# Attention with decay and a bilinear FFN on one core: idle matmuls at the start, f loaded through ScalarE's queue, eight transposes of P moved from DMA to the tensor engine, a new order

## The chip, the core and the metric

The kernel runs on one core of one Trainium2 chip. The core has a tensor engine (PE; its weight loads are shown apart as PEld), a vector engine (DVE), a scalar engine (ACT), GpSimd (POOL) and SyncE (SP), which issues most DMAs; 16 DMA engines move the data. The metric is the device time of one execution in microseconds (us); lower is better.

## What is computed

Forgetting attention over 8 batches of 8 heads, 576 tokens each, head dimension 64, then a bilinear FFN on the 4608 tokens:

```python
scores = scale * np.matmul(q, k.transpose(0, 1, 3, 2))
log_f = np.log(np.clip(f, 0.0001, 1.0))
cum = np.cumsum(log_f, axis=-1)
decay = cum[:, :, :, None] - cum[:, :, None, :]
scores = np.where(causal, -1000000000.0, scores + decay)
attn = softmax(scores)                       # max, exp, sum, divide
out  = np.matmul(attn, v)                    # 8 x 8 x 576 x 64
x = out.transpose(0, 2, 1, 3).reshape(4608, 512)
a = x @ w_a                                  # 512 x 1536
b = x @ w_b
return a * b @ w_out                         # 1536 x 512
```

The inputs are float32 in HBM (q, k, v, f, w_a, w_b, w_out); the kernel works in fp16 on PE with float32 sums.

## The kernel before

Two heads make a pair; t = 0 to 31 counts the pairs, four to each batch b. Queries and keys of a pair are cut into blocks of 128 (i = 0 to 3) and a last block of 64 (i = 4). The work is written as a list of small operations, each with one engine, the operations it needs and a function that emits its instructions. The order in which they are emitted is not worked out at run time: it is a list of operation numbers (`ORDER`) with a letter for each operation that more than one engine could do (`CHOICE`). Each engine runs its own instructions strictly in that order, and so does each DMA queue.

- **Start.** `f_load` (L170) loads f in two DMAs on SP's queue. `constants` (L72) makes an identity matrix `ident16` on POOL (L73) and then masks and selection vectors. `clip`, the logarithm (ScalarE, L212), `scan` (L187) and the copies into `crow` turn f into the running sum of log f, in two pieces of columns. q and k of batch 0 are loaded (L270), cast to fp16 (L242, L244), transposed by PE against the identity (`pe_transpose`, L285; PSUM tile `psT`) and copied out by DVE or ACT (`pe_evict`). v is loaded at L251 and cast into `nv`.
- **Scores.** `qk_group` (L417) multiplies q and k blocks into PSUM tile `sc`. For batch 0 the decay and the mask are added by matmuls (`crow`, `pick`, `neg`, `low`); for later batches the decay is added on DVE (L540) from `spread`. For pairs 4 to 7 PE broadcasts the decay (`spread_mm`, L482, tile `scd`: one 128x512 matmul each); later pairs load it by DMA (L493).
- **Softmax.** DVE takes the maxima (L514 in batch 0), ACT the exponentials (L567, L571), DVE the reciprocals (L579, L581), POOL the products P times 1/sum (L589). P of a pair lies in `PA` (blocks i = 0 to 2; for the first two batches in two parts, A0 for i = 0, 1 and A1 for i = 2, six 128x128 blocks each) and `PB` (i = 3, 4).
- **Transposes of P.** In batch 0 (`PEP`) PE transposes P (`pe_tr`, L609, tile `psP`) and DVE or ACT copies it out (`pe_tr_evict`). From batch 1 on a DMA does it (`do_tr`, L603, on SP's queue). For the first two batches the transposed A parts lie in the later half of `xT`, a buffer that is free until then; so `xT<-PA` in the profile is such a transpose.
- **P times V.** `do_pv` (L631) and `do_pv4` (L647) into tile `pv` (one buffer), copied to `xT`.
- **FFN.** Cuts of tokens: 256, 256, 256, 384, then 512 each. `ff_mm` (L914) makes `psa` and `psb` in 12 blocks, ACT copies `psa`, DVE multiplies (L925), `ff_out` (L934) makes `pso`, which is copied and stored (L954). A cut needs the attention of all its tokens, from all four pairs. POOL issues the weight loads (L392).

The branch that chooses between PE and DMA for the transposes is `if b in PEP:` (L822); what sets the engine order is lines 1036 to 1160.

Of the kernel before, what the change touches and what calls it, by code (L numbers as in the profile page):

```python
# [9 lines left out]
FP32 = mybir.dt.float32  # L10
# [15 lines left out]
def kernel(  # L26
# [11 lines left out]
    nc = tc.nc  # L38
# [30 lines left out]
    ident16 = perm.tile([128, 128], FP16, tag="ident16", name="ident16")  # L69
    warm = perm.tile([128, 1], FP32, tag="warm", name="warm")  # L70

    def constants():  # L72
        make_identity(nc, ident16)  # L73
        for x in pickh:
            nc.gpsimd.memset(x, 0.0)
        for m in range(4):
            x = slice(32 * m, 32 * m + 32)
# [71 lines left out]
    def take(op, tag):  # L149

        users = [op]
        op.takes.append((tag, users))
        return users
# [16 lines left out]
    def f_load(half):  # L170
        rows = f.rearrange("b (h p) s -> h b p s", h=2)
        nc.sync.dma_start(out=cw["f"][64 * half:64 * half + 32, :], in_=rows[half])
# [27 lines left out]
    o_f = [Op("SP", 0.5, lambda _, half=half: f_load(half), prio=-310, land=0.3, name=f"ldf{half}") for half in range(2)]  # L200
# [3 lines left out]
    o_c = Op("POOL", 4.5, lambda _: constants(), prio=-300)  # L204
# [99 lines left out]
    PEP = tuple(range(1))  # L304

# [372 lines left out]
    def attention(t, base):  # L678
# [12 lines left out]
        if not direct:  # L691
            if t in PSPREAD:
# [3 lines left out]
                for h in range(2):  # L696
                    bm = Op("PE", 512 * COLS, lambda _, h=h: spread_mm(t, h), crow_ops[0] + crow_ops[1] + [bc0] + bcs, prio=prio(0) - 5, mode="full", name=f"bm{t}")
                    su = take(bm, "ff")
                    bc = Op(None, {"ACT": 0.59, "DVE": 0.69}, lambda e, h=h: spread_ev(e, t, h), [bm, bc0], prio=prio(0) - 5, name=f"bc{t}")
                    su.append(bc)  # L700
                    bcu.append(bc)
                    bcs.append(bc)
            else:
# [115 lines left out]
        for part in norms:  # L819
            lo, hi = BLOCKS[part]  # L820
            p = prio({"A0": 0, "A1": 1}.get(part, 2))
            if b in PEP:  # L822
# [210 lines left out]
    for n in cuts:  # L1033
# [3 lines left out]
        0 1 26 20 32 38 3-6 27 28 11 7 2 29 30 12 21 22 8 10 9 13 14 19 33 34 23 24 31 25 18 61 64 35 70 106 15  # L1037
# [7 lines left out]
        178 1739 173 256 174 1741-1743 272 1740 1744 275 265 266 179 273 1745 104 139 276 289 283 282 290 105  # L1045
# [3 lines left out]
        1762-1764 280 287 60 288 221 222 226 484 264 328 385 329 293 150 330 294 472 473 231 1765 334 1766 384  # L1049
        378 339 232 373 1767 1768 379 386 233 194 1769 1771 389 390 340 388 387 485 295 234 1770 1773 341 1774  # L1050
        342 391 392 1775 336 195 1772 1776 274 296 297 393 303 304 474 1777-1779 239 298 475 299 305 1780 338
# [4 lines left out]
        1802 427-429 439 440 435 1804 313 1805 1807 1806 1809 1808 1810 314 424 434 1811 442 441 1812 1813  # L1056
# [4 lines left out]
        528 519-521 529 546 1837 545 413 414 552 1838 530-532 553 547 507 533 514 513 579 676 1786 458 671 460  # L1061
# [6 lines left out]
        608 616 594 636 617-619 614 643 644 620 637 610 684 622 609 596 621 615 1893-1896 638 645 639 646 1898  # L1068
# [10 lines left out]
        1969-1971 798 895 896 816 897 797 1972 787 788 811 794 821 822 1973 823 1974 838 1976 1978 892 836 791  # L1079
        826 827 846 847 818 1975 1977 824 828-830 907 898 903 953 848 854 856 1979 849 1980 842 839 1982 812 806  # L1080
        831 819 813 908 820 832 825 853 855 841 860 917 1983 1981 844 867 861 857 1984 1985 868 837 1986 840 850
        852 899 904 858 1987-1989 863 834 833 1990 1992 843 910 1994 869 954 905 1991 862 1996 1993 918 926 872
# [5 lines left out]
        986 955 980 987 982 1000 984 990 991 1100 992 993 951 952 2023 2018 1002 2026 2029-2031 1003 1006 2034  # L1088
# [102 lines left out]
```

## Time and profile before

| what | value |
|---|---|
| median of 3 runs | 418.04 us (415.95 to 419.21) |
| profiled execution, device time | 413.75 us |
| its span | 412.0 us |
| its granted clock of PE | 0.998 |
| PE busy | 388.2 us (94%) |
| DVE busy | 302.8 us (73%) |
| ACT busy | 277.8 us (67%) |
| POOL busy | 265.1 us (64%) |

The profile's page gives busy time by engine for one execution; "busy" for PE counts a matmul from issue to its modelled end, so neighbouring matmuls overlap. The page also cuts the span into 40 slices of 10.3 us; each digit is a tenth of the slice:

```profile
PE   1698999999999999899999999999999999999995
DVE  5987998897889859777798789768878793432331
ACT  2877898885987668876786778777877673231230
POOL 6899797877796786875967787767865845000000
```

PE is nearly full from the third slice to the end, the other three until about slice 32; what is left after that is FFN alone. A finer view of any stretch can be asked: instructions in order of time, who waited for whom, and the busy time of each engine in chosen stretches.

### The profile page before, as it was taken

The page shows a single profiled execution, that of the slowest core. Times are in us where ns is not written, and L with a number is a line of the kernel's source. Part 1 is how long each engine was busy: PE and PEld are TensorE (multiplying, and loading weights), DVE is VectorE, ACT ScalarE, POOL GpSimd, SP SyncE. Part 2 cuts the span into 40 slices and gives each one's busy share as a digit, 9 for nine tenths or more (in the row PEclk, how much of TensorE's full clock was granted, in tenths as well). Part 3 has the DMA queues.
Part 4 walks back from the last instruction along what each step waited for, and adds up shares of the span by engine and source line. Part 5 has one row for each costly group of instructions (what it writes and reads, how often), then busy time and mean ns, then how long its engine had stood idle before and what let it go on. Part 6 is the DMA issues. An engine that isn't in the chain of part 4 may idle for free. (4 is left out here: it accounts for less than half of the span.)

```text
span 412.0 us, 10863 instructions
## 1 busy us (share of the span) xinstructions
PE 388.2 (94%) x3788; PEld 209.6 (51%) x3788; DVE 302.8 (73%) x1011; ACT 277.8 (67%) x788; POOL 265.1 (64%) x490
## 2 busy tenths in 40 slices
PE   1698999999999999899999999999999999999995
PEld 1456675756756544444445444444454444444552
DVE  5987998897889859777798789768878793432331
ACT  2877898885987668876786778777877673231230
POOL 6899797877796786875967787767865845000000
PEclk9999999999999999999999999999999999999999
DMA  6999999999999999999999999996996729200102
GB/s 245 200 240 215 227 197 244 211 230 256 257 215 233 288 218 246 221 240 244 232 208 283 298 190 211 266 223 210 186 222 205 156 56 180 84 1 11 68 0 103
DMA packets 153575, 80.56 MB, mean 196 GB/s; under 512 B 130736, under 2 KB 133552, under 8 KB 153520
## 3 DMA queue, kind: packets, MB, share of 16 engines
q1 hardware_dynamic: 149616, 75.02, 78.5%
q0 software_dynamic: 3760, 4.72, 7.0%
q8 instruction: 29, 0.48, 0.5%
q14 instruction: 26, 0.21, 0.2%
q10 hardware_dynamic: 144, 0.13, 0.1%
HBM read 52.05 MB, written 9.58 MB: 150 GB/s over the span
## 5 line engine op out<-in xcount | busy, mean ns | idle before, releaser
L540 DVE CUSTOM_DVE_ANT_0 S<-sc,spread 64x576 f32<-64x576 f32 (+4 forms) x232 | 126.4, 562 | 13.3 <-PE sc L417 6.1
L914 PE MATMUL psa<-xT,wa 128*128 128x512 f16 (+2 forms) x528 | 115.3, 341 | 1.3 <-ACT a L240 0.8
L914 PE MATMUL psb<-xT,wb 128*128 128x512 f16 (+2 forms) x528 | 115.3, 341 | 0.4 <-DVE PTB L244 0.2
L240 ACT CAST a<-psa 128x512 f16<-128x512 f32 (+2 forms) x132 | 66.5, 505 | 57.2 <-PE psa L914 50.5
L925 DVE TENSOR_TENSOR ht<-psb,a 128x512 f16<-128x512 f32 (+2 forms) x132 | 77.4, 590 | 34.2 <-PE psb L914 26.3
L589 POOL TENSOR_SCALAR PA<-PA,st 128x256 f16<-128x256 f16 (+2 forms) x192 | 90.3, 480 | 18.3 <-DVE st L581 12.3
L934 PE MATMUL pso<-wout,ht 128*128 128x512 f16 x432 | 100.0, 380 | 0.0
L571 ACT ACTIVATE PA<-S,st 128x256 f16<-128x256 f32 (+2 forms) x168 | 84.6, 506 | 8.1 <-DVE st L540 8.1
L589 POOL TENSOR_SCALAR PB<-PB,st 128x512 f16<-128x512 f16 (+1 forms) x96 | 67.6, 712 | 24.3 <-DVE st L581 13.1
L914 PEld LDWEIGHTS <-wa 128*128 128x128 f16 x528 | 49.0, 98 | 42.1 <-issue 4.4
L914 PEld LDWEIGHTS <-wb 128*128 128x128 f16 x528 | 49.1, 98 | 40.2 <-issue 1.8
L934 PEld LDWEIGHTS <-ht 128*128 128x128 f16 x432 | 39.8, 98 | 45.6 <-issue 0.9
L571 ACT ACTIVATE PB<-S,st 128x512 f16<-128x512 f32 x56 | 40.4, 721 | 11.1 <-DVE st L540 9.7
L417 PE MATMUL sc<-kT,qT 64*128 64x128 f16 (+4 forms) x384 | 35.8, 274 | 3.1 <-ACT kT L240 1.4
L240 ACT COPY osb<-pso 128x512 f32<-128x512 f32 (+1 forms) x19 | 10.8, 569 | 32.3 <-DMA out_dram<-osb 15.7
L571 ACT ACTIVATION_READ_ACCUMULATOR PA<-S,st 128x1 f32 x168 | 32.3, 192 | 0.0
L244 DVE CAST xT<-pv 128x512 f16<-128x512 f32 (+1 forms) x40 | 23.1, 576 | 6.6 <-PE pv L631 6.4
L244 DVE COPY osb<-pso 128x512 f32<-128x512 f32 (+1 forms) x18 | 12.1, 674 | 20.8 <-PE pso L934 14.9
L631 PEld LDWEIGHTS <-nv 128*64 128x64 f16 x640 | 19.5, 110 | 13.1 <-issue 9.8
L581 DVE RECIPROCAL st<-st 128x2 f32<-128x2 f32 x128 | 18.9, 157 | 9.9 <-ACT PB L571 5.2
L417 PEld LDWEIGHTS <-qT 64*128 64x128 f16 (+1 forms) x384 | 13.8, 96 | 23.0 <-issue 15.6
L567 ACT ACTIVATE PB<-S,st 128x576 f16<-128x576 f32 x28 | 21.7, 775 | 4.4 <-issue 2.3
(92 smaller groups left out, 454.2 us busy)
## 6 DMA issues: line engine op xcount, KB each, us to landing
spread<-cum_d SPq DMA_DIRECT2D x24, 576.0 KB, 5.6
out_dram<-osb SPq DMA_DIRECT2D x35, 256.0 KB, 2.8
q<-in_q_dram SPq DMA_DIRECT2D x15, 576.0 KB, 6.4
k<-in_k_dram SPq DMA_DIRECT2D x15, 576.0 KB, 5.9
v<-in_v_dram SPq DMA_DIRECT2D x32, 256.0 KB, 5.7
wout<-in_moe_w_out_dram POOLq DMA_DIRECT2D x3, 512.0 KB, 7.8
v<-in_v_dram SPq DMA_DIRECT2D x8, 128.0 KB, 4.4
wa<-in_moe_w_a_dram POOLq DMA_DIRECT2D x2, 512.0 KB, 10.3
```

The costliest lines, as they stand in the source:

```text
L240: nc.scalar.copy(out=out_, in_=in_)
L244: VEC[e].tensor_copy(out=out_, in_=in_)
L417: nc.tensor.matmul(out=dst, lhsT=lhsT, rhs=rhs, start=start, stop=stop, skip_group_check=True)
L540: nc.vector.tensor_tensor_reduce(out=o, in0=x, in1=y, scale=-1.0, scalar=3e38, op0=ADD, op1=MIN, accum_out=m)
L567: nc.scalar.activation(out=p_blocks(t, 4), in_=T[("s" if direct else "z", t, 4)], func=EXP, bias=st[:, 8:9], scale=sign, accum_out=st[:, 1 ...
L571: nc.scalar.activation(out=p_blocks(t, i)[:, :, h, :], in_=(T[("s", t, i)][:, h, :] if direct else T[("z", t, i)][:, h * n:h * n + n]).rea ...
L581: nc.vector.reciprocal(out=st[:, 20 + 2 * i:22 + 2 * i], in_=st[:, 10 + 2 * i:12 + 2 * i])
L589: VEC[e].tensor_scalar(out=p, in0=p, scalar1=st[:, c:c + 1], scalar2=1.0, op0=MUL, op1=MUL)
L631: nc.tensor.matmul(out=o[HP[h], 128 * i:128 * i + 128], lhsT=vt[:, j, pr + NP * h, :], rhs=pt[:, base_blk[i] + 2 * block_at(t, i, j) + h, ...
L914: nc.tensor.matmul(out=p[:, 0:n], lhsT=w16[:, db, 128 * fb:128 * fb + 128], rhs=xTflat[db][:, t0:t0 + n], start=(db == 0), stop=(db == 3))
L925: nc.vector.tensor_tensor(out=ht[:, 0:n], in0=T.pop(("psb", t0, fb))[:, 0:n], in1=T.pop(("a16", t0, fb))[:, 0:n], op=MUL)
L934: nc.tensor.matmul(out=o, lhsT=T[("ht", t0, fb)][:, 128 * tb:128 * tb + 128], rhs=wout16[:, fb, :], start=(fb == 0), stop=(fb == 11))
```

## The change

Five things change.

1. The identity matrix becomes an operation of its own on POOL (`identity`), ahead of the other constants.
2. Twenty operations `wake` are added on PE. Each is two matmuls of 64 rows of the identity against one identity column, broadcast to 512 columns, into a tile of tag `pv`; nothing reads it. They need only the identity. In the new order six stand ahead of the first transpose of q, two more ahead of k's, two ahead of the first scores, and the other ten between the operations of batch 0, the last one ahead of the third P times V product (`pv1`).
3. f is loaded on ScalarE's queue (two DMAs ahead of everything else on ScalarE). The first load on SP's queue is now the 64-token rest of v (`ld0v4`), then q, k, k, q and v of batch 0.
4. For pairs 4 to 7 (batch 1), parts A0 and A1 are transposed by PE: eight `do_tr` go, eight `pe_tr` of six blocks with eight `pe_tr_evict` come (four on ACT, four on DVE). Part B of these pairs stays with the DMA.
5. `ORDER` and `CHOICE` are new for the whole kernel. Among the choices, one k cast of batch 0 goes from ACT to POOL, the rest of v of batch 0 (`ca0v2`) from POOL to DVE, and some evictions between DVE and ACT; the weight loads on POOL stand at other places.

The branch added for `MASKP` inside the `PSPREAD` case is never taken (pairs 4 to 7 are not in `MASKP`).

```diff
+    def identity():
+        make_identity(nc, ident16)
+
+    def wake(n):
+        x = ps.tile([128, 512], FP32, tag="pv", bufs=1, name="wake")
+        for _ in range(n):
+            nc.tensor.matmul(out=x, lhsT=ident16[0:64, :], rhs=ident16[0:64, 0:1].to_broadcast([64, 512]),
+                             start=True, stop=True, skip_group_check=True)
+
     def constants():
-        make_identity(nc, ident16)
         for x in pickh:
...
-        nc.sync.dma_start(out=cw["f"][64 * half:64 * half + 32, :], in_=rows[half])
+        nc.scalar.dma_start(out=cw["f"][64 * half:64 * half + 32, :], in_=rows[half])
...
-    o_f = [Op("SP", 0.5, lambda _, half=half: f_load(half), prio=-310, land=0.3, name=f"ldf{half}") for half in range(2)]
+    o_f = [Op("ACT", 0.85, lambda _, half=half: f_load(half), prio=-310, land=0.3, name=f"ldf{half}") for half in range(2)]
...
-    o_c = Op("POOL", 4.5, lambda _: constants(), prio=-300)
+    o_i = Op("POOL", 1.2, lambda _: identity(), prio=-301, name="ident")
+    o_c = Op("POOL", 3.3, lambda _: constants(), [o_i], prio=-300, name="const")
+    for n in range(20):
+        o = Op("PE", 0.427, lambda _: wake(2), [o_i], prio=-290, mode="row", name=f"wake{n}")
+        o.prev = [last_wake] if n else []
+        last_wake = o
+        take(o, "pv")
...
     PEP = tuple(range(1))
+    PEQ = {(t, x) for t in range(4, 8) for x in ("A0", "A1")}
...
-            if b in PEP:
+            if b in PEP or (t, part) in PEQ:
...
     ORDER = """
-        0 1 26 20 32 38 3-6 27 28 11 7 2 29 30 12 21 22 8 10 9 13 14 19 33 34 23 24 31 25 18 61 64 35 70 106 15
...
+        2 0 1 69 47 41 53 59 24-26 32 27 33 48 49 28 42 43 29 31 30 34 3-9 50 10 11 39 51 40 44 12 45 46 52 35
...
     CHOICE = """
-        DDPPDDAADDADAPDAPPDDPPPDDAADDDADDDDADDAAAAAADADDADDDDAAAAADADAAAAAAAADADDADAAAAAAADADAADADAAAADADAAA AAA
+        DDPPDDAADDAAPPDAPPDDPDPDDDADDDADADAADDAAAAAADADAAADDDAADDDDADAAAAADAAADAADDAAADDDAAAAAADAAADAAADDA
+        DAAADDDADAA
```

More of the change, by code (lines that the diff above doesn't have):

```diff
@@ L702, in attention @@
                     bcs.append(bc)
+                if t in MASKP:
+                    mc = Op("POOL", 0.9, lambda _: mask_copy(t), list(bcs), prio=prio(0) - 4, name=f"mc{t}")
+                    ml = Op("POOL", 0.42, lambda _: mask_last(t), [mc], prio=prio(3) - 0.5, name=f"ml{t}")
+                    bcu.extend([mc, ml])
             else:
@@ L1036 @@
     ORDER = """
-        0 1 26 20 32 38 3-6 27 28 11 7 2 29 30 12 21 22 8 10 9 13 14 19 33 34 23 24 31 25 18 61 64 35 70 106 15
[7 rows of a table removed]
-        178 1739 173 256 174 1741-1743 272 1740 1744 275 265 266 179 273 1745 104 139 276 289 283 282 290 105
[3 rows of a table removed]
-        1762-1764 280 287 60 288 221 222 226 484 264 328 385 329 293 150 330 294 472 473 231 1765 334 1766 384
-        378 339 232 373 1767 1768 379 386 233 194 1769 1771 389 390 340 388 387 485 295 234 1770 1773 341 1774
-        342 391 392 1775 336 195 1772 1776 274 296 297 393 303 304 474 1777-1779 239 298 475 299 305 1780 338
[4 rows of a table removed]
@@ L1056 @@
-        1802 427-429 439 440 435 1804 313 1805 1807 1806 1809 1808 1810 314 424 434 1811 442 441 1812 1813
[4 rows of a table removed]
-        528 519-521 529 546 1837 545 413 414 552 1838 530-532 553 547 507 533 514 513 579 676 1786 458 671 460
[6 rows of a table removed]
-        608 616 594 636 617-619 614 643 644 620 637 610 684 622 609 596 621 615 1893-1896 638 645 639 646 1898
[10 rows of a table removed]
-        1969-1971 798 895 896 816 897 797 1972 787 788 811 794 821 822 1973 823 1974 838 1976 1978 892 836 791
-        826 827 846 847 818 1975 1977 824 828-830 907 898 903 953 848 854 856 1979 849 1980 842 839 1982 812 806
@@ L1081 @@
-        831 819 813 908 820 832 825 853 855 841 860 917 1983 1981 844 867 861 857 1984 1985 868 837 1986 840 850
-        852 899 904 858 1987-1989 863 834 833 1990 1992 843 910 1994 869 954 905 1991 862 1996 1993 918 926 872
[5 rows of a table removed]
-        986 955 980 987 982 1000 984 990 991 1100 992 993 951 952 2023 2018 1002 2026 2029-2031 1003 1006 2034
-        975 988 2032 1102 983 1010 1005 989 1108 1109 976 994 996 977 1055 1011 1024 1025 1017 2027 1012 2036
-        2038 1013 2035 1026 1019 1018 968 2037 1027 1020 2039 969 1008 2040 1007 1031 1028 1032 2041-2043 1033
[9 rows of a table removed]
@@ L1100 @@
-        1176-1178 1180 1181 1169 1182 1188 1310 1189 1184 1191 1183 1158 1185 1159 1134 2093 2094 1172 2095 1190
-        1195 1196 1192 2097 1303-1305 1168 1160 1171 2098 1313 2091 1255 1197 1165 1140 1186 1200 2099 2100 1201
-        1193 1116 1202-1204 1206 2102 2104 1212 1216 2106 2103 1220 1228 1198 1199 2108 2107 2110 1222 1221 1223
-        2111 2105 1234 1235 1227 1205 1179 1194 1318 1162 1161 1327 2112 1213 2114 2113 1215 2109 1187 1319 1229
-        1237 1236 2115-2117 1238 1314 1219 1214 2118 2119 1218 1207 1208 1315 1217 2120 1241 1242 1256 1211 2121
@@ L1105 @@
-        1265 1316 1230-1232 1317 1243 2122 1258 2124 2123 1328 1224 1226 1240 1239 1266 1246 1244 1245 1273 1247
[6 rows of a table removed]
-        1349 1429 1357 1324 1365 1384 1366 1367 1363 1512 1358 2160-2162 2154 1516 2163 1377 1513 1380 2159 1343
-        1350 1351 1386 1514 2165-2167 1344 1517 1379 1392 1378 1368 1369 1385 1398 1370 1399 1515 1391 1387 1401
[12 rows of a table removed]
-        2233 1587 1590 2234 1588 1589 1608 1598 1592 1615 1578 1554 1559 2235 2236 1605 1610 2238-2240 1616 1609
[3 rows of a table removed]
-        1656 1655 2261 1607 1689 1599 1619 1625 1626 2262-2264 1638 2266 1634 1635 2265 1661 1662 2268 2267 1657
[4 rows of a table removed]
@@ L1135 @@
-        1674 1673 2291 2292 1723 1721 1724 2293 2296-2298 2301 1675 2294 1676 2295 2290 2299 2302 1725 2303 1726
-        1677 1678 2304 2305 2300 2306-2308 2310 2309 2311 2312 2314 2316 2313 2315 2317-2320 1727 2322 2321
-        2323 2324 2326 2325 2327 2328 1728 2330 2329 2331 2332 2334 2336 2333 2335 2338 2340 2337 2339 2341 2342
-        2344 2343 2345-2348 2350 2349 2351-2356 2359-2362 2357 2363 2358 2364-2366 2369 2370 2367 2371-2374 2376
-        2375 2378 2377 2380 2379 2382 2381 2384 2383 2386 2388 2387 2385 2389 2390 2392 2391 2394 2393 2396 2395
@@ L1140 @@
-        2398 2397 2400 2399 2402 2401 2404 2403 2406 2405 2408 2407 2410 2409 2412 2411 2414 2413 2416 2415 2418
-        2420 2419 2422 2421 2417 2423 2424 2427 2425 2428 2426 2368 2429 2432 2430 2433-2435 2431 2437 2436 2438
+        2 0 1 69 47 41 53 59 24-26 32 27 33 48 49 28 42 43 29 31 30 34 3-9 50 10 11 39 51 40 44 12 45 46 52 35
+        54 288 55 36 60 37 13 82 14 85 61 91 65 56 15 127 16 289 57 130 58 86 136 290 92 87 93 131 62 83 132
+        137 138 17 291 18 292 72 74 71 66 63 88 94 97 64 340 99 98 172 96 175 89 181 139 341 19 342 128 142 133
@@ new lines @@
+        140 95 70 141 176 182-184 186 90 67 177 20 343 21 344 178 173 185 76 180 179 73 135 134 113 100 187 114
[3 rows of a table added]
+        1759 148 1761 154 118 111 145 149 235 79 112 150 155 156 151-153 275 237 1762 1764 205 1763 1765 174 193
+        206 147 157 146 81 119 1766 162 279 280 286 120 1767 194 163 1768 1769 199 276 123 195 278 293 296
+        303 304 124 297 200 277 1770-1772 294 298 310 1773 311 1774 160 125 126 1775 299 161 196 273 198 197 312
+        281 306 305 283 282 219 164 168 1776 238 201 169 1777 236 1778 165 244 300 302 202 239 1779 240 284 207
@@ new lines @@
+        1780 1782 208 307 308 1781 345 348 245 1783 313 1784 1785 241 1786 209 210 356 397 400 349 407 355 1787
+        350 213 214 1788-1790 250 170 314 251 246 401 402 357 1791-1793 408 358 351 409 243 309 301 242 80 287
+        316 329 252 359 330 1794 253 171 352 346 1795 410 360 247 501 513 403 398 1796 1797 362 363 414 315 354
+        285 404 405 502 353 361 254 1798 331 215 255 216 415 1799 1800 332 1802 260 261 365 364 1803 417 416
+        1804 258 1801 1805 295 324 411-413 406 317 503 1806 504 505 318 319 381 514 1807 1808 433 320 382 1809
[3 rows of a table added]
@@ new lines @@
+        1825 423 511 424 339 512 450 334 1826 335 1827 452 453 425 1828-1830 460 1831 430 1832 1833 454 431 466
[12 rows of a table added]
+        643 631 713 644 632 657 1922 647 1923 646 648 665 666 673 649-651 1924 661 714 667 1925 679 680 715 658
[3 rows of a table added]
+        735 747 1950 1952 1954 1951 753 1953 754 1955-1958 1960 1962 755 758 748 1959 759 740 1961 670 711 677
[5 rows of a table added]
+        864 1991 1992 825 917 822 918 843 919 844 824 839 832 1993 1995-1997 1999 845 838 2000 827 1998 823
[8 rows of a table added]
+        1007 977 1008 959 953 986 2049 2050 991 1004 997 1005 978 979 1130 1123 987 1009-1011 988 1131 1012 1006
@@ new lines @@
+        1038 2051 1014 1124 2053 2054 1127 990 1015 984 1029 1016 1128 1031 1019 1039 1129 1040 1020 1017 1021
+        1041 2055 2058-2060 2063 1042 2064 1022 980 981 2052 1032 1035 2061 1034 2047 1132 1074 1013 998 1018
[5 rows of a table added]
+        1106 1107 1082 1134-1136 1076 1105 2093 1079 2094 1111 2095 1108 1112 2096-2099 1149 1113 1114 1153 1157
[7 rows of a table added]
+        1347 1356 2135 2137 1245 2136 1263 1264 1252 1242 1244 1243 1221 2138-2140 1265 1259 1228 1215 1294 1343
+        1209 1234 1247 2141 2143 1208 1235 1348 1222 1285 1223 1216 1237 1354 2145 2144 2147 1266 2142 1236 2125
@@ new lines @@
+        1340 1270 1271 2146 2148 1246 1287 1344 1260-1262 1240 1345 1272 1295 1267 2149 1346 1253 1255 1275 1296
+        2151 2153 1297 2152 1273 1277 1276 2154 2150 1254 1268 1298 1274 1269 2155 1288 1291 1349 2156 1341 1278
+        1351 1302 1350 1303 1299 1279 2157 1309 1290 2159 2160 1305 1304 2161 2163 2164 1311 1310 1289 1352 1281
+        1280 1355 1300 1282 1283 1293 2162 2165 1312 2167 2168 1306 2158 1316-1318 2166 1313 2169 2171 1292 1359
+        1286 2173 2172 2175 2170 1321 1323 1322 1324 1325 2176 2177 1360 1363 2179 2178 1319 2180 1540 1402 1314
@@ new lines @@
+        1307 1315 1357 1367 1369 1327 1353 1366 1301 1308 1374 2174 2181 1375 1361 1368 1362 1381 1382 1376
+        1383 1384 2130 1448 2182 1365 2184-2186 1388 1328 1389 1370 1377 1390 1320 1326 1329 1403 1364 1405 2189
+        1378 1379 1358 1385 1412 1458 1387 1541 1413 1421 1393 1391 1371 1372 1415 1423 1395 2190-2192 2183 1545
+        1414 1394 1396 2187 1406 1409 1542 1392 2188 1494 1550 2194-2196 1543 1408 1420 1427 1407 1428 2199 2200
[9 rows of a table added]
+        1533-1536 1517 1573 1570 1577 1529 1530 1585 1591 1592 2250 1579 1594 1587 1593 2252-2254 1575 2257 2198
[3 rows of a table added]
@@ new lines @@
+        2269-2271 1619 1620 2273 1637 2272 2274 1638 1634 2275 1639 2276 1646 2277 2278 1647 1629 1614 1565 1609
[5 rows of a table added]
+        2305 1715 1716 2307 2309 2306 1733 2308 1735 1723 1734 1736 1725 2310 1717 1740 2311-2313 2315 2316 1741
+        1730 2314 1737 1713 1731 1681 1710 1732 1742 1743 1745-1747 1724 1738 1739 2317 1748 2318 1749 1703 1702
+        2320 2321 1744 1752 1751 1750 1753 2322 2325 2326 1704 2327 2330 1705 2323 2319 2324 2328 2331 1754 2332
+        1755 2333 2334 2329 2335 2337 2339 2336 2338 2341 2343 1756 2340 2342 2345 2347 2344 2346 2348-2357 2359
@@ new lines @@
+        2358 2360 2361 2363 2365 2362 2364 2366-2371 2373 2372 2374-2385 1757 2388 1706 2389 2390 1707 2391 2386
+        2392 2387 2393-2395 2398 2399 2396 2400 2401 2397 2402 2403 2405 2404 2407 2406 2409 2408 2411 2410 2413
+        2412 2415 2417 2416 2414 2418 2419 2421 2420 2423 2422 2425 2424 2427 2426 2429 2428 2431 2430 2433 2432
+        2435 2434 2437 2436 2439 2438 2441 2440 2443 2442 2445 2444 2447 2449 2448 2451 2450 2446 2452 2453 2456
+        2454 2457 2455 2458 2461 2459 2462-2464 2460 2466 2465 2467
@@ L1142 @@
     """
     CHOICE = """
-        DDPPDDAADDADAPDAPPDDPPPDDAADDDADDDDADDAAAAAADADDADDDDAAAAADADAAAAAAAADADDADAAAAAAADAADADADAAAADADAAA AAA
+        DDPPDDAADDAAPPDAPPDDPDPDDDADDDADADAADDAAAAAAADADAAADDDAADDDDADAAAAAADAAADAADDAAADDDAAAAAADAAADAAADDA
+        DAAADDDADAA
     """
```

136 rows, old and new, of the table ORDER are left out of this document.

## The prediction

> **What bounds the kernel now.** I read the coarse view first: busy time of each engine in stretches of the span (columns: the stretch and its length, then PE, PEld, DVE, ACT, POOL busy us with counts, granted clock, DMA share, GB/s).
>
> ```profile
> 0.00:12.00 12.00, 2.19 (x43) 1.53 (x45) 7.03 (x15) 4.61 (x8) 7.68 (x35) 1.00 0.78 246
> 12.00:22.00 10.00, 7.49 (x100) 4.45 (x97) 9.24 (x20) 8.73 (x33) 9.28 (x16) 1.00 0.87 199
> 22.00:29.00 7.00, 6.88 (x83) 4.42 (x84) 5.81 (x14) 5.48 (x22) 6.92 (x15) 1.00 1.20 228
> 29.00:34.00 5.00, 4.50 (x75) 2.84 (x73) 4.15 (x14) 4.30 (x11) 4.93 (x10) 1.00 1.11 255
> 34.00:40.00 6.00, 5.06 (x70) 3.68 (x66) 4.52 (x11) 4.33 (x11) 5.98 (x10) 1.00 1.01 201
> 40.00:70.00 30.00, 29.23 (x445) 20.31 (x447) 27.39 (x99) 26.61 (x80) 24.82 (x39) 1.00 1.18 220
> 70.00:100.00 30.00, 27.33 (x330) 18.10 (x323) 25.67 (x104) 22.62 (x71) 22.78 (x39) 1.00 1.15 238
> 100.00:340.00 240.00, 237.57 (x2280) 121.10 (x2278) 195.57 (x698) 182.37 (x521) 176.91 (x319) 1.00 0.96 222
> ```
>
> From 34 us on PE is full but for 0.9 us in 34 to 40, 0.8 in 40 to 70, 2.7 in 70 to 100 and 2.4 in 100 to 340. The chain that ended last is PE's FFN matmuls (L914, L934). So two things set the time: when PE's dense work begins, and how much work and how many holes come after. Before 34 us PE idles 12.9 us (9.8 + 2.5 + 0.1 + 0.5), while POOL is full from 13 us on. Next, PE in order of time (start, us, then what):
>
> ```profile
> 20.82 0.61 PE L482 MATMUL scd<-crow,pick 128*128 128x512 f16 x1
> 22.12 0.51 PE L417 MATMUL sc<-kT,qT 64*128 64x384 f16 x2 [0.69 <-ACT PA L571]
> 27.53 0.61 PE L482 MATMUL scd<-crow,pick 128*128 128x512 f16 x1
> 30.85 0.39 PE L482 MATMUL scd<-crow,pick 128*128 128x512 f16 x1
> 32.54 0.58 PE L285 MATMUL psT<-ident,q 64*128 64x64 f16 x18 [0.22 <-POOL q L242]
> 34.24 0.61 PE L914 MATMUL psa<-xT,wa 128*128 128x256 f16 x4
> ```
>
> The same matmul takes 0.61 us up to 27.53 and 0.39 at 30.85, so the array runs slow through the head, which the granted-clock column (1.00) doesn't show. From 22.12 to 28.5 PE ran without a break before it sped up. The first FFN matmul (34.24) follows q's transpose (32.54), which waited for POOL. What POOL did just before:
>
> ```profile
> 26.80 0.66 POOL L392 DMA_DIRECT2D wa<-in_moe_w_a_dram  x1
> 27.46 1.05 POOL L244 CAST nv<-v 128x1024 f16<-128x1024 f32 x1
> 28.60 2.76 POOL L589 TENSOR_SCALAR PA<-PA,st 128x256 f16<-128x256 f16 x6
> 31.34 1.15 POOL L242 TENSOR_SCALAR q<-q 128x1152 f16<-128x1152 f32 x1
> ```
>
> Last, who PE waited for between 34 and 100 us (us in total, times, longest):
>
> ```profile
> PE pv L631 <- DMA xT<-PA: 1.4, 3, 0.8
> PE psP L609 <- POOL PB L589: 0.8, 1, 0.8
> PE psa L914 <- ACT a L240: 0.8, 1, 0.8
> PE pv L647 <- DVE xT L244: 0.5, 1, 0.5
> ```
>
> The 1.4 us are the DMA transposes (L603) that the change replaces.
>
> **The change, part by part.** The profiled execution took 413.75 us, 412.0 of it span; the median of the three runs is 418.04, 4.3 above. I sum on the profiled execution and carry the difference to the median.
>
> *f on ScalarE's queue, a v load first on SP's.* The two f issues held SP from 0.81 for 1.65 us, q's came at 2.51. Now one half-size v load (some 0.5 us) precedes q, whose issue moves 1.2 us ahead; k, k, q move with it. The DMA engines are full from 4 us on (share 0.96 to 1.06), so about half, 0.6 us, reaches the landings. ScalarE spends the 1.65 us before its table load (1.28): its first LN can begin at about 3.9, and it began at 5.00 waiting for f, so this is covered; uncovered it would cost 1.65.
>
> *New order in the head.* By rows: f clips at 5.0 to 5.7, q casts (1.33 for two) to 7.0 against 7.61, the first scan and the k casts to 8.5 against 9.6. ScalarE loses one k cast (0.62) that stood ahead of the kT evictions, so the first scores start near 9.8 against 11.49 and their maxima near 11 against 12.86. POOL takes that cast, and until the last norm of the fourth head pair it loses the 1.05 us v cast (now on DVE) and one weight issue (0.65). Adding its rows from the k landing (9.7 against 10.36), with the norms behind, that norm ends near 28 against 30.3. But q's cast for the second batch now has one norm more ahead of it (0.58): it ends near 30.8 against 32.49. It releases PE's transpose, and the first FFN matmul follows as before: **start −1.7 us**. Bounds: 0 (POOL had no break to save) and −3.0 (PE never the limit either).
>
> *Idle matmuls.* 40 of 512 columns. No row has them. At full speed four 512-column matmuls take 0.86 us, so 0.43 for each pair; slow, twice that. Six pairs come before the first transpose: 5.1 us from about 1.4, done at 6.5, when q's cast is due: cost 0 to 0.2. The other fourteen are strewn over PE's queue up to about 30 us: 6.0 us at full speed. Their cover is PE's idle time in the head (3.1 us after 12, 2.9 between 6.9 and 12) and what real work gives back at the higher speed (half of the 14.4 us busy from 12 to 29, 7.2). So no cost if the array is fast; if it is not, they are 12.0 us against 6.0 of cover. With the six pairs, the transpose and two more pairs back to back from 1.4 on, the run before it speeds up is as long as the 6.4 us above: full speed by about 8 us.
> [...]
>
> *Transposes by PE.* P's blocks of pairs 4 to 7, parts A0 and A1: eight DMA transposes go, eight groups of six PE transposes come. At full speed such a group began at 45.68 and the next work at 46.12: 0.44 each, **+3.5 us** of PE work in its dense time (0.51 each, the row's length, would be 4.1). Eight evictions of 0.55 (DVE) or 0.80 (ACT) come, with DVE 88% and ACT 82% busy from 40 to 100. SP gets rid of eight issues of 1.3 us, with what is queued behind them.
>
> *Holes from 34 to 100.* 4.4 us. Gone should be the DMA transposes' waits (1.4) and the wait for PB (0.8: that norm now follows directly on four weight issues, near 36 against 39.9); the rest are waits for evictions after a late transpose. I take three quarters: **−3.3 us**; bounds 0 and −4.4. From 100 on the order is as dense as PE allows; its 2.4 us can shrink or double: 0, ±2.
>
> *The clock's luck.* The profiled execution sped up at 28.5. Where a run speeds up later, 5 us of PE work between 29 and 34 take up to 4.9 us more, and the median lies 4.3 above. Bounds 0 and −4.3, since an early rise takes all of it out. Nothing in one trace shows how much; I take **−1.7**, nearer to nothing, because DMA timing could spread the runs as well.
>
> Sum: −1.7 + 3.5 − 3.3 − 1.7 = −3.2 us; 418.04 − 3.2 = **414.8**.
>
> **Rivals.**
> *All of the 4.3 us is the late clock* (chance 0.25). For it: the profiled run is faster than all three timed ones. Against: nothing seen. −1.7 + 3.5 − 3.3 − 4.3 = −5.8: 412.2. [...]
> *The transposes give nothing back* (0.14). Place: the FFN's third cut (psa from 97.7 us), which needs all of the second batch's first blocks. The eight evictions (5.4 us) stand in ACT and DVE queues that are over 80% full; it decides if they come later than the DMA did (3.7 us from issue to landing). Then the holes stay, and half of the 5.4 is added: −1.7 + 3.5 + 2.7 = +4.5: 422.5, slower.
> *The head gains nothing* (0.14): POOL, full from 13 us, keeps its pace, and the clock is no matter. 0 + 3.5 − 3.3 = +0.2: 418.2.
> *The idle matmuls don't raise the clock* (0.05): 12.0 − 6.0 = 6.0 later, + 3.5 − 3.3: 424.2. Against: 6.4 us of unbroken work did raise it at 28.5.
>
> **How the numbers follow.** The likeliest case, the sum, has 0.42; its own range is 412 to 417.5. A change of 1% (4.2 us: 413.9 and 422.2) is about what a measurement can tell. Faster: 0.33 of the sum's chance and nine tenths of the clock rival's, 0.37. Slower: half of the eviction rival's and all of the last, 0.13. Within 1%: 0.50. The range, 410.5 to 420, leaves out the eviction rival, the slow-clock rival and a tail below: a little under 0.2.
>
> **What would show it.** Matmul groups at full length from about 8 us (a 512-column scd of 0.39, not 0.61); first scores near 10, first psa near 32.5; no "pv <- DMA xT<-PA" wait, and less than 1.5 us of PE idle between 70 and 100; 48 more psP transposes of PA. The prediction is wrong if scd is still 0.61 at 15 us, if psa starts later than 34, if PE waits for xT evictions in 60 to 100, or if the holes after 100 grow past 4 us.

## The result and the profile after

| | before | changed |
|---|---|---|
| median of 18 runs each | 416.31 us | 420.99 us |
| range | 415.36 to 419.33 | 417.94 to 422.99 |
| ratio to before, 95% interval | | 1.0097 (1.0075 to 1.0119) |
| profiled execution, device time (span) | 413.75 (412.0) | 422.31 (420.3) |

The change made the kernel 1% slower, about 4 us. The forecast was 414.8, range 410.5 to 420.0.

The same stretches as before the change (stretch and its length, then PE, PEld, DVE, ACT, POOL busy us with counts, granted clock, DMA share, GB/s), of the changed kernel:

```profile
0.00:12.00 12.00, 8.45 (x37) 2.54 (x38) 4.46 (x12) 4.27 (x7) 7.30 (x37) 1.00 0.72 234
12.00:22.00 10.00, 9.94 (x108) 4.80 (x103) 6.97 (x14) 5.71 (x20) 7.23 (x12) 1.00 0.82 135
22.00:29.00 7.00, 7.00 (x41) 2.52 (x41) 4.58 (x12) 4.59 (x17) 3.04 (x9) 1.00 0.65 147
29.00:34.00 5.00, 4.55 (x58) 3.09 (x55) 3.99 (x10) 2.70 (x12) 4.51 (x9) 1.00 1.00 209
...
70.00:100.00 30.00, 29.61 (x382) 20.38 (x381) 29.01 (x110) 25.86 (x73) 22.68 (x39) 1.00 0.90 225
100.00:340.00 240.00, 234.94 (x2262) 121.12 (x2261) 195.68 (x694) 178.03 (x513) 177.15 (x321) 1.00 0.99 224
```

The bound in the head has changed engines. From 12 to 29 us PE is full (16.9 of 17 us, 14.4 before), while POOL fell from 16.2 to 10.3 us and DVE from 15.1 to 11.6: they now wait for PE. From 70 to 100 us PE is fuller than before (29.6 against 27.3), as hoped; from 100 to 340 its idle time doubled, from 2.4 to 5.1 us.

PE in order of time (start, us, what):

```profile
1.44 6.35 PE L78 MATMUL wake<-ident 64*128 64x512 f16 x12 [1.44 <-POOL ident masks.py:199]
9.56 0.85 PE L299 MATMUL psT<-ident,q 64*128 64x64 f16 x18 [1.78 <-DVE q L256]
...
27.60 0.61 PE L497 MATMUL scd<-crow,pick 128*128 128x512 f16 x1
28.14 0.60 PE L78 MATMUL wake<-ident 64*128 64x512 f16 x1
...
33.42 0.38 PE L497 MATMUL scd<-crow,pick 128*128 128x512 f16 x1
...
39.64 0.69 PE L299 MATMUL psT<-ident,q 64*128 64x64 f16 x18 [0.56 <-POOL q L256]
...
41.39 0.61 PE L933 MATMUL psa<-xT,wa 128*128 128x256 f16 x4
```

Three things are to be seen. The twelve idle matmuls ahead of q ran without a break from 1.44 to 7.8 us, and still the 512-column scd took 0.61 us at 27.60; the last slow matmuls stand at 30.9 us (28.2 before). q's first transpose began at 9.56 instead of 6.87. And the first FFN matmul began at 41.39 instead of 34.24, 7.2 us later. Why q came late is seen on DVE:

```profile
8.64 0.53 DVE L192 TENSOR_SCALAR cum_f<-cum_f 96x256 f32<-96x256 f32 x2 [6.38 <-DMA cum_f<-in_f_dram]
9.09 0.82 DVE L256 TENSOR_SCALAR q<-q 128x512 f16<-128x512 f32 x2
```

The first clip of f waited until 8.64 us for f to land, and q's casts stood behind it. In the kernel before, the same line was:

```profile
4.67 0.29 DVE L184 TENSOR_SCALAR cum_f<-cum_f 96x256 f32<-96x256 f32 x1 [2.41 <-DMA cum_f<-in_f_dram]
```

POOL, full before, now waits for DVE, and DVE for PE's scores (first a line of POOL's work in order of time, then one of who waited for whom up to 42 us: us in total, times, longest):

```profile
25.80 0.72 POOL L604 TENSOR_SCALAR PA<-PA,st 128x128 f16<-128x128 f16 x2 [3.32 <-DVE st L596]
...
DVE st L529 <- PE sc L432: 5.3, 5, 1.6
```

Who PE waited for (us in total, times, longest), three lines of the changed kernel's list:

```profile
PE pv L646 <- DMA PTB<-PB: 1.3, 2, 1.0
PE psb L933 <- DVE ht L944: 1.3, 1, 1.3
...
PE pv L646 <- DMA PTA<-PA: 0.7, 1, 0.7
```

The waits for xT<-PA are gone; others have come, for DMA transposes of later parts of P (`PTB`, `PTA`), most of them after 105 us.

From the first psa to the first psa of the eleventh FFN cut PE took 350.1 us before (34.2 to 384.3) and 351.5 after (41.4 to 392.9). So most of the loss arose ahead of the first psa: 7.2 us in the two profiled executions, of which that of before (413.75) lay 2.6 below its median of 18 runs and that of after (422.31) 1.3 above its own.

### The profile page after: what moved, and what is told of

Its sections match the earlier page's. It is cut to its first block, busy times and chain, and to the rows that moved or that the text cites. A ratio compares the mean times of both kernels' runs of the same rounds, so it can differ in the third digit from the quotient of the medians.

```text
span 420.3 us, 11012 instructions
## 1 busy us (share of the span) xinstructions
PE 404.3 (96%) x3876; PEld 216.0 (51%) x3876; DVE 306.7 (73%) x1017; ACT 280.1 (67%) x790; POOL 264.1 (63%) x490
## 4 chain that ended last, share of the span: by engine, by line
PE 69%; DMA 15%; POOL 5%; DVE 4%; issue 3%; ACT 2%; ACTq 0%; SPq 0%; DVEq 0%; POOLq 0%
PE pso L953 17%; PE psb L933 17%; PE psa L933 17%; PE sc L432 7%; DMA PTB<-PB 5%; PE pv L646 4%; DMA wb<-in_moe_w_b_dram 3%; DMA PTA<-PA 2%; PE wake L78 2%; PE psT L299 2%; DMA q<-in_q_dram 2%; DMA spread<-cum_d 2%; POOL PB L604 2%; DMA cum_f<-in_f_dram 1%; POOL PA L604 1%
## 5 line engine op out<-in xcount | busy, mean ns | idle before, releaser
L604 POOL TENSOR_SCALAR PA<-PA,st 128x128 f16<-128x128 f16 (+2 forms) x192 | 90.3, 480 | 24.7 <-DVE st L596 22.0
L604 POOL TENSOR_SCALAR PB<-PB,st 128x512 f16<-128x512 f16 (+1 forms) x96 | 67.4, 708 | 24.2 <-DVE st L596 14.4
L432 PE MATMUL sc<-kT,qT 64*128 64x128 f16 (+4 forms) x384 | 37.8, 273 | 0.8 <-ACT PA L586 0.4
L514 POOL TENSOR_SCALAR_AFFINE_SELECT spread<-spread 128x768 f32<-128x768 f32 x24 | 20.8, 867 | 8.1 <-DMA spread<-cum_d 8.0
L258 POOL CAST nv<-v 128x1024 f16<-128x1024 f32 (+1 forms) x23 | 20.4, 889 | 5.8 <-DMA v<-in_v_dram 3.6
```

Of the source, the lines that this page charges most:

```text
L258: VEC[e].tensor_copy(out=out_, in_=in_)
L432: nc.tensor.matmul(out=dst, lhsT=lhsT, rhs=rhs, start=start, stop=stop, skip_group_check=True)
L514: nc.gpsimd.affine_select(out=c[:, :, 0:SM].rearrange("p h (j k) -> p h j k", k=128), in_=c[:, :, SM:2 * SM].rearrange("p h (j k) -> p h j ...
L604: VEC[e].tensor_scalar(out=p, in0=p, scalar1=st[:, c:c + 1], scalar2=1.0, op0=MUL, op1=MUL)
```

## The experiments

Times are medians; each ratio is against the kernel before on the same chip. 0.1% is 0.42 us. "The rise" is the moment from which PE's matmuls run at the full rate (a 128x512 scd in 0.39 us instead of 0.61).

**Without the idle matmuls.** The body of `wake` is left out.

```diff
     def wake(n):
-        x = ps.tile([128, 512], FP32, tag="pv", bufs=1, name="wake")
-        for _ in range(n):
-            nc.tensor.matmul(out=x, lhsT=ident16[0:64, :], rhs=ident16[0:64, 0:1].to_broadcast([64, 512]),
-                             start=True, stop=True, skip_group_check=True)
+        return
```

> The changed kernel without its 40 idle matmuls; everything else as it is. Theory A (they ran at the slow rate, 0.43 us each, and those strewn over PE's queue held up the work behind them): PE gets back about half of the 12 us that the last fourteen pairs took, the first psa comes 3 to 6 us sooner than 41.4 us, and the time falls by 3 to 6 us, to 415 to 418. Theory B (f came late, the idle matmuls fill waits that are there anyway): the time moves by less than 1 us. Theory C (they did bring the rise of the clock forward): the rise comes later than 30.9 us and the time grows.

Measured: ratio 0.9999 (0.9960 to 1.0038), 416.91 us; the first psa at 36.3, the rise at 30.4 us. Theory A holds, against B and C: the idle matmuls cost about 1%, 4 us, the whole of what the change lost.

**f back on SP's queue, and f alone on ScalarE's.** The first undoes one part of the change, the second does it alone in the kernel before.

```diff
-        nc.scalar.dma_start(out=cw["f"][64 * half:64 * half + 32, :], in_=rows[half])
+        nc.sync.dma_start(out=cw["f"][64 * half:64 * half + 32, :], in_=rows[half])
```

> The changed kernel with the two loads of f back on SP's queue, where they now come first; the idle matmuls stay on ScalarE's side of nothing else. Theory B (on ScalarE's queue f landed at 8.6 us instead of 4.7, and DVE holds the q casts behind it): the first clip of f starts at 4.5 to 5 us, q's first transpose at 6.5 to 7.5 instead of 9.6, the first psa 2 to 3 us sooner, the time 2 to 3 us lower. Theory A (PE, slow and full from 9.6 to 31 us, sets the head): PE only starts its queue sooner by those 2.5 us, which gives the same 2 to 3 us at most; if instead POOL or DVE set the head, under 1 us.

Measured: ratio 1.0060 (1.0026 to 1.0094). f's clip began at 4.64 us, but q's casts only at 7.71, waiting for q: the v load and f now both went ahead of q on one queue. The first psa came at 37.5, 3.9 us sooner; in this execution the rise also came sooner, at about 21 us, so not all of that is f's. Against the change's 1.0097 it is about 1.5 us, but the two intervals overlap, so this gain is not shown beyond the noise.

> The kernel before with one thing changed: the two loads of f go through ScalarE's queue, order unchanged. Theory F (f shares the DMA engines with q, k, k, q on SP's queue and lands last): the first clip of f starts at 7 to 9 us instead of 4.7; DVE stands at it with q's casts behind, so q's first transpose comes 1.5 to 3 us later than 6.87, the first psa 1.5 to 3 us later than 34.2, and the time grows by 1.5 to 3 us (ratio 1.004 to 1.007). Rival (f was late in the changed kernel only because the small packets of the v load went first): the clip starts near 5 us, the time falls or stays within 1 us.

Measured: ratio 1.0068 (1.0035 to 1.0101), 2.8 us slower; the first psa at 35.6, though the rise came at 21.4 us already in this trace. On DVE:

```profile
8.37 0.29 DVE L184 TENSOR_SCALAR cum_f<-cum_f 96x256 f32<-96x256 f32 x1 [6.11 <-DMA cum_f<-in_f_dram]
8.58 0.82 DVE L242 TENSOR_SCALAR q<-q 128x512 f16<-128x512 f32 x2
```

Theory F holds; the rival falls, since here no v load went ahead. In all six traces with f on ScalarE's queue the clip began between 8.3 and 9.2 us, in the eleven with f on SP's between 4.4 and 5.8. The issue time was saved (q's load is issued at 0.81 us in this run, at 2.51 before), but the small load that had gone first now went among the large ones. The records of the DMA packets show it: f's 64 packets had all ended at 4.0 us in the kernel before; here they end at 7.5 us, when 712 packets of the same size from SP's queue are through as well. The second of f's two loads sent none before 6.1 us; why it stood back that long stays open.

**The form of the idle matmul.** Three forms of the idle matmul in the changed kernel, all else as it is: 128 rows instead of 64; 64 rows of ones; 128 rows of ones (a tile that DVE sets at the start). The edit of the first:

```diff
-            nc.tensor.matmul(out=x, lhsT=ident16[0:64, :], rhs=ident16[0:64, 0:1].to_broadcast([64, 512]),
+            nc.tensor.matmul(out=x, lhsT=ident16, rhs=ident16[:, 0:1].to_broadcast([128, 512]),
```

> The idle matmuls with all 128 rows of the identity instead of 64, same column of the identity (one 1 and 127 zeros) as the moving operand. If the clock counts how much of the array is in use, twice the rows raise it: 512-column matmuls at 0.22 us pitch before 10 us. If it counts values that are not zero, nothing changes: slow to about 31 us.

> The changed kernel with idle matmuls of 64 rows as it has them, but with ones in both operands in place of the identity. With 128 rows of the identity (one 1 in the moving column) the first rise came at 6.6 us. If rows in use are what counts: the first twelve, 1.4 to 8 us, stay at 0.42 us pitch to the end. If values count too: they speed up before 8 us.

> The idle matmuls with 128 rows and ones in both operands (a tile of ones, set by DVE), so that every cell multiplies something. If values or rows in use raise the clock: scd (128x512) takes 0.39 instead of 0.61 us from 10 us on, the idle matmuls cost half, the first psa comes 4 to 6 us sooner than 41.4, the time is 415 to 417. If the clock rises by something else (a fixed time, real work only): no change, rise at about 31 us, time within 1 us of the changed kernel.

Measured: with 128 rows of the identity the first full-rate matmul came at 6.7 us, 414.68 us in one run. With 64 rows of ones the first twelve stayed slow to the end; the rise came at 25.7 us, 419.38 us in one run. With 128 rows of ones it came at 6.3 us; ratio 0.9989 (0.9956 to 1.0022). So in these runs the early rise went with the rows and not with the values: 128 rows had it with one 1 and 127 zeros (6.7 us) as with ones (6.3 us), and 64 rows did not, with the identity (30.9 us) or with ones (25.7 us). All three forms have 128 columns of weights, so rows can't be told from the share of the array that is in use. Against the changed kernel without idle matmuls (0.9999) neither form with 128 rows shows a gain. Over all runs, full rate came at 4.9 to 7.2 us with 128 rows, in seven traces of seven, and with 64 rows not before 21 us, in four of four. The run with 128 rows of the identity, in two stretches:

```profile
7.00:9.00 2.00, 0.24 (x2) 0.00 (x0) 0.24 (x2) 0.00 (x0) 0.49 (x2) 1.00 1.02 348
10.00:13.00 3.00, 2.92 (x35) 1.18 (x32) 2.95 (x7) 1.88 (x3) 1.92 (x3) 0.50 0.69 168
```

PE was idle from 7.3 to 9.7 us (f was late here too), and from 10 to 13 us the granted clock, the last column but two, reads 0.50. The four idle matmuls that began at 10.46 us took 2.11 us, the four at 13.09, where the column reads 1.00 again, 1.27. So after a rise the column does show the slow rate, as 0.50; ahead of the first rise it reads 1.00 in every stretch of the kernel before and of the changed one, with the matmuls slow (scd 0.61 us). The fall came at 9.7 us and the next rise at 13.1, 3.4 us on; with 128 rows of ones, PE idle from 6.9 to 9.7, the fall came at 9.3 and the next rise at 16.1. In the changed kernel PE worked nearly without a break for 21 us (21.2 of 21.4 us busy from 9.5 to 30.9, 18.3 of them on 64 rows), and its matmuls stayed slow all that time.

**The head mended.** f on SP's queue with 128-row idle matmuls; then also the v load behind q, k, k, q.

```diff
-        2 0 1 69 47 41 53 59 24-26 ...
+        2 0 1 47 41 53 59 69 24-26 ...
```

> The changed kernel with idle matmuls of all 128 rows of the identity and f back on SP's queue. Theory (both mishaps of the head are then mended): clip at 4.6 us, q's casts near 7.7 as with f on SP alone (the v load still goes ahead of q), full rate from 13 us at the latest, the first psa 33.5 to 35, the time 412 to 415 where the kernel before has 416.5. Rival (POOL and DVE set the head whatever PE does): psa near 36, time within 1 us of the kernel before.

> As the run with 128 rows and f on SP, and the 64-token rest of v loads after q, k, k, q instead of ahead of them. If its issue (0.7 us) and its packets of 256 bytes delay q: q's casts start at 6.3 to 6.6 instead of 7.7, the first psa about 1 us sooner, time 0.5 to 1.5 us lower. If q's landing is not the limit: no change.

Measured: 0.9935 (0.9905 to 0.9965), first psa at 34.0; and 0.9945 (0.9914 to 0.9975), first psa at 33.1, q's casts at 6.56. Both are faster than the kernel before. The v load's place moved q by 1.1 us in the trace; in the time the two can't be told apart.

**What each is worth in the mended head.** The last kernel with 128-row, without, and with 64-row idle matmuls; a first comparison, across chips, left intervals that overlap; the second was made on one chip.

> The kernel with f on SP's queue and the v load behind q, k, k, q, without any idle matmul. It prices the early rise of the clock alone, against the same kernel with 128-row idle matmuls (ratio 0.9945 to the kernel before, first psa at 33.1). If PE's rate matters in the head: rise between 21 and 31 us, first psa 34 to 35.5, 1 to 2.5 us slower than with them (ratio 0.997 to 1.001). If POOL and DVE set the head: psa at 33 to 33.5 and the same time, ratio 0.993 to 0.996; then all that the mended kernel gains is order and loads.

> The kernel with f on SP's queue, the v load behind q, k, k, q, and 128-row idle matmuls, again, now on the same chip as the same kernel without them. If the early rise of the clock is worth something: at least 1 us faster than without. If not: within 0.5 us. Against the kernel before: ratio 0.992 to 0.997.

> The same kernel without idle matmuls. Early rise worth something: ratio to the kernel before 0.997 to 1.001, with a wider spread of times, since the rise comes between 19 and 31 us and may be followed by a fall. Early rise worth nothing: ratio 0.992 to 0.997, as with them.

> The same kernel with the idle matmuls of 64 rows that the change has. They ran slow in three traces and stand in PE's queue: against none, the first psa 2 to 5 us later and the time 2 to 4 us higher (ratio to the kernel before 1.002 to 1.007). If they only filled waits: as without them.

| idle matmuls, mended head | median us | ratio to before (95%) | full rate from | first psa |
|---|---|---|---|---|
| none, first comparison | 414.56 | 0.9987 (0.9951 to 1.0023) | 18.9 us | 34.0 |
| none | 412.71 | 0.9921 (0.9891 to 0.9951) | 27.8 us | 33.9 |
| 128 rows | 411.45 | 0.9912 (0.9882 to 0.9942) | 4.9 us | 33.0 |
| 64 rows | 416.58 | 1.0049 (1.0013 to 1.0085) | 21.4 us | 37.1 |

The last three rows were measured together, on one chip. The 64-row ones cost 3.9 us against none. The 128-row ones gave 1.3 us in the median and 0.9 us in the trace's first psa, but the two intervals overlap: the early rise is worth something between 0 and 2 us, and the gain is not shown beyond the noise. The first two rows are one kernel on two chips. Their ratios lie 0.7% apart, so a difference of that size between ratios from different chips need not be an effect of the code; what is compared on one chip is firmer. Their traces also show that the rise varies from run to run, 18.9 us in one and 27.8 in the other, and the first fell back to half rate at 22 and at 49.5 us, 3.4 us each. The 128-row kernel's head, and the line of the 64-row one that answers to its first:

```profile
1.44 5.22 PE L78 MATMUL wake<-ident 128*128 128x512 f16 x12 [1.44 <-POOL ident masks.py:199]
6.92 0.29 PE L299 MATMUL psT<-ident,q 64*128 64x64 f16 x8 [0.27 <-DVE q L256]
...
33.00 0.61 PE L933 MATMUL psa<-xT,wa 128*128 128x256 f16 x4
```

```profile
1.44 5.94 PE L78 MATMUL wake<-ident 64*128 64x512 f16 x11 [1.44 <-POOL ident masks.py:199]
```

With 128 rows, twelve end at 6.66, ahead of q's transpose; with 64, eleven end at 7.4 and the twelfth, between two parts of q's transpose, at 7.8.

**The idle matmuls alone in the kernel before.** Its order with 22 of them, 128 rows: twelve right behind the identity, four behind each of the first transposes of q and k, two in the first scores.

```diff
     def constants():
         make_identity(nc, ident16)
+        wake(12)
...
+        if b == 0 and half == 0:
+            wake(4)
...
+        if t == 0 and g == 0:
+            wake(2)
```

> The kernel before, order unchanged, with 18 idle matmuls of 128 rows: twelve ahead of q's first transpose, four behind each of the first transposes of q and k, two in the first group of scores (22 in all with these). If the early rise is worth something by itself: full rate from 6 to 8 us on, the first psa 0.5 to 2 us sooner than 34.2, time 1 to 3 us lower (ratio 0.993 to 0.998). If POOL sets the head there, psa near 34 and no change in the time beyond 0.5 us. If the clock falls back in the waits of 1 to 1.5 us between 8 and 13 us, scd is 0.61 at 15.7 again and nothing changes.

Measured: ratio 1.0061 (1.0026 to 1.0095): slower, against the expectation. The rise came at 7.2 us, but PE paused from 14.0 to 15.9 us and the clock fell again at 17.4; stretches of that run:

```profile
8.00:17.00 9.00, 5.98 (x113) 3.12 (x106) 8.25 (x17) 7.55 (x23) 5.19 (x9) 1.00 1.15 250
18.00:27.00 9.00, 7.66 (x76) 4.69 (x72) 7.78 (x18) 6.45 (x27) 8.94 (x21) 0.50 1.09 254
```

The first psa came at 34.3, as in the kernel before: in that order, full rate up to 17 us bought nothing. The loss shows later, in one wait of 2.9 us for a DMA transpose (xT<-PA) from 96 to 99 us, and behind it the clock fell once more, from 99.3 to 102.7 us. Why that transpose came later stays open.

**The transposes.** In the mended 128-row kernel the eight went back to DMA, at the places where PE had them; and the kernel before got them alone, each with its eviction, where it had issued the DMA.

```diff
     def pe_tr(t, part, lo, hi):
+        if (t, part) in PEQ:
+            do_tr(t, part)
+            return
...
     def pe_tr_evict(e, t, part, lo, hi):
+        if (t, part) in PEQ:
+            return
```

> As the run with the v load moved, and the eight transposes of P of pairs 4 to 7 go back to DMA, issued where PE had them; PE's 48 transposes and their eight evictions are gone. Theory (they cost PE 3.5 us of dense time, and save holes of about 3 us): the time moves by less than 1.5 us, PE work falls by 3.5 us and waits of PE for the transposed blocks come back with 2 to 4 us between 50 and 105 us. Rival (nothing came back for them): 3 to 4 us faster. Rival (they pay): 2 us or more slower.

```diff
-            tr = Op("SP", 1.3, lambda _, part=part: do_tr(t, part), norms[part], prio=p,
+            def tr_fn(_, part=part, lo=lo, hi=hi):
+                if 4 <= t < 8 and part in ("A0", "A1"):
+                    pe_tr(t, part, lo, hi)
+                    pe_tr_evict(e, t, part, lo, hi)
+                else:
+                    do_tr(t, part)
+
+            tr = Op("SP", 1.3, tr_fn, norms[part], prio=p,
```

> The kernel before with only the eight transposes of P of pairs 4 to 7 given to PE, each with its eviction right behind it where the DMA was issued; nothing else moves. Theory (3.5 us of PE work against holes of about that size): within 1.5 us of the kernel before, no wait of PE for xT<-PA, the third FFN cut (psa from 97.7 us) 0 to 3 us sooner. Rival (they cost PE's work and give nothing back): 3 to 4 us slower. Rival (they are the gain, as taking them away from the mended kernel suggested): 2 to 5 us faster.

In the second edit `e` is ACT or DVE, as in the change.

Measured: with DMA in the new order 1.0203 (1.0134 to 1.0272), 2.6% slower than the same kernel with PE transposes (four runs only); PE then waited 3.6 us for k and q casts and 6.4 us for PTB<-PB. The transposes there stand at PE's places in SP's queue, with loads behind them, so this may not be their price alone. Added to the old order: 1.0075 (1.0043 to 1.0108), 3.1 us slower; no wait for xT<-PA is left, but the third FFN cut starts at 101.5 instead of 97.7 us, 3.4 us longer after the first psa. PE's idle time from 34 to 97.5 us is 4.4 us in both traces: in place of the 1.4 us for xT<-PA stand waits for the evictions, two lines of which are

```profile
PE psP L609 <- DVE xT L244: 0.6, 1, 0.6
...
PE pv L631 <- DVE xT L244: 0.3, 1, 0.3
```

So taken alone they cost what they add to PE's work. In the mended kernel that idle time, from 34 to 100 us, is 1.4 to 1.6 us with or without 128-row idle matmuls: the new order, made around the transposes, gets back most of what they cost.

## Why the prediction was wrong, step by step

- **Idle matmuls: the step that failed.** "With the six pairs, the transpose and two more pairs back to back from 1.4 on, the run before it speeds up is as long as the 6.4 us above: full speed by about 8 us." In its place: full speed at 30.9 us with idle matmuls on 64 rows. I took unbroken PE time as what counts; that was an estimate from one stretch (22.12 to 28.5) that mixed work on 64 and on 128 rows, and the changed kernel's 21 us of work on end without a rise went against it. The mechanism that followed was the rival with 0.05: idle matmuls that stay slow and stand in PE's queue. It gave +6.0 us for the start; their removal measured about 4 (1.0097 to 0.9999, and 416.58 to 412.71 in the mended head). The six pairs ahead of q were mis-sized as well, 6.35 us and not 5.1, which q's late cast hid.
- **f on ScalarE's queue: failed too.** I costed the issue (1.65 us, covered) and the landing of q, and let f land when it had landed before. Its clip began 4 us later, and DVE, in order, held q behind it. Alone it costs 2.8 us in the kernel before; from the changed kernel (1.0097) to the same with f on SP and v behind (1.0049), 2 us, though on another chip.
- **New order in the head: right way, too large, and not the order's alone.** The working gave −1.7, the first psa near 32.5. With 128-row matmuls, f on SP and v behind q it came at 33.0 and 33.1, −1.2 us; with the v load still first at 34.0, and without the early rise at 33.9, less than 0.4 us each. In the change as it is, it came at 41.4. In the old order the early rise gave nothing (34.3), so the gain takes the order, the loads and the clock together.
- **Transposes by PE, and holes: right in sum, not in parts.** +3.5 and −3.3 made +0.2 for the dense stretch; it measured +1.4 (350.1 to 351.5 us), and 347.8 to 351.2 in the three traces of the mended kernel with 128 rows. The holes from 34 to 100 us shrank from 4.4 to 3.0 us in the change (those of 70 to 100 from 2.7 to 0.4) and to 1.4 to 1.6 in the mended head, near the −3.3 of the sum. But holes after 100 us grew by 2.6, past the 2 allowed; in the mended kernel they are 2.5 to 5.3 us, so this varies from trace to trace. Alone, in the old order, the transposes cost 3.1 us and gave nothing back.
- **The clock's luck: too large.** −1.7 was taken; an early rise measured 1.3 us in the mended head, not shown beyond the noise, and nothing in the old order. Of the 4.3 us between the profiled execution and the first three runs, 1.7 was those three: 18 runs of before have a median of 416.31. What makes up the other 2.6 stays open. The rival that put all of it down to the clock falls.
- **The other rivals.** The evictions (transposes give nothing back, third cut late) were seen in the old order alone, not in the new one. "The head gains nothing" is not what happened: it lost.

Three of the listed signs of being wrong showed at once: scd at 0.61 us past 15 us, psa later than 34, and holes after 100 us of 5.1.

## What to carry to other kernels

Before idle matmuls are strewn over a queue, look in traces for a form that full rate follows early: here it came with 64 rows not before 21 us, and they cost 1%; with 128 rows it came by 7.2 us, but gave no gain clear of the noise (in the old order they came out 0.6% slower). A small load that the first work waits for did better here ahead of the large ones on one queue than beside them on another (f's clip at 4.67 against 8.37 us); and before a DMA is moved, ask what stands behind its consumer in an engine's order. When an order is made anew around a change, parts taken out of it or put into the old one can cost what the whole does not: the mended kernel (ratio 0.9912) has the transposes that alone cost 0.75%.

## What was not expected of the hardware

- With idle matmuls of 64 rows and 512 columns, twelve on end (the changed kernel's took 6.35 us) and more strewn behind, the array stayed slow for 19 us or more in four traces of four; with 128 rows full rate came within 3.5 to 5.7 us of their start in seven of seven, whether the operands were ones (6.3 us) or nearly all zeros (6.7 us).
- The rise didn't always hold: in five traces the granted clock fell to 0.50, seven times in all, for stretches of 3.4, 6.8 or 10.2 us. Shortly ahead of each fall PE had paused for 1.3 to 2.9 us in one go (from 7.3 to 9.7 us ahead of the fall at 9.7, from 14.0 to 15.9 ahead of that at 17.4, from 96 to 99 ahead of that at 99.3); after a pause of 1.45 us in another trace (128 rows, f on SP's queue) the clock did not fall.
- The granted-clock column reads 1.00 ahead of the first rise, while the same matmul (128x512) takes 0.61 instead of 0.39 us.
- f, 144 KB in two loads, was ready 3.7 us later from ScalarE's queue than from SP's (its clip began at 8.37 against 4.67 us, nothing else changed).
